# Fewer tiles transposed on TensorE in the first token steps of a two-layer mixer kernel

## The chip, the core and the metric

The kernel runs on one core of a Trainium2 chip. The metric is the device time of one execution in microseconds (us); lower is better. Engines are named as the profile names them: PE (TensorE, matrix multiply; PEld is its weight load), DVE (VectorE), ACT (ScalarE), POOL (GpSimd), and SP, whose queue (SPq) issues every DMA of this kernel in order. Each engine works through its own instructions in the order in which they were written, and waits at an instruction until what that needs is there.

## The reference

Two blocks alternate, A B A B, on x of 2048 tokens by 512 features in float32, each added to its input after a layer norm.

```python
def _A_ref(x, wqkv, wo):                 # linear attention, 32 heads of 16
    q, k, v = ...                        # from x @ wqkv
    phi = lambda t: jnp.where(t > 0, t + 1, jnp.exp(t)) + 1e-6
    pq, pk = phi(q), phi(k)
    kv = jnp.einsum("bhsd,bhse->bhde", pk, v)
    z = jnp.einsum("bhsd->bhd", pk)
    num = jnp.einsum("bhqd,bhde->bhqe", pq, kv)
    den = jnp.einsum("bhqd,bhd->bhq", pq, z)[..., None] + 1e-6
    return ... (num / den) ... @ wo

def _B_ref(x, w_in, w_sp, b_sp, w_out):  # gated mixer over tokens
    z = _gelu(jnp.einsum("bsd,df->bsf", x, w_in))
    z1 = z[..., :Fh]
    z2 = _layernorm(z[..., Fh:], axis=-1)
    g = jnp.einsum("ts,bsf->btf", w_sp, z2) + b_sp[None, :, None]
    return jnp.einsum("bsf,fd->bsd", z1 * g, w_out)
```

## The kernel before

The tokens are cut into 16 tiles of 128 rows (NT). Every float32 matrix product is made of three matmuls: each operand is split into a high half (a rounded copy, made on ScalarE, L119) and a low half (the rest, a subtraction on VectorE, L122); `mm3` (L133 to L135) multiplies high by high, high by low, and low by high. The low half of the left operand is first read by the third matmul.

The schedule is written out by hand: the order of the calls is the order of the instructions on each engine. Each of the two layers (A and then B) has three phases: P1 (keys, queries and the sum over tokens), a short transition, P2 (queries times the summed matrix, first residual, the layer norm and the two input projections of B), and P4 (the product over tokens and the output projection). The change is in P2.

P2 runs in steps s = 1 to 18; in a step several tiles are at different stages. For a tile i:

- `a(i)` multiplies the query features with the summed keys on GpSimd (L571); `a2_den` forms the denominators on VectorE (L583 to L585); `a2_mul` divides (VectorE, L592). The result is the q tile. `qturn.store(i)` then takes it on its way to be transposed.
- `b_high(i)` and `b_low(i)` get the transposed q tile and split it (L119, L122).
- `c(i)` is the matmul group that multiplies it with the 512 x 512 matrix W2: 12 matmuls. `c2` adds x (VectorE, L624), `c_stats` takes mean and variance (VectorE L196 and L198, then three small GpSimd instructions, L200 to L203), and `c3` stores x, normalises it on ScalarE (L209) and hands the y row to `xturn.store(i)`.
- `d_high(i)` and `d_low(i)` get the transposed y row and split it.
- `e(i)` multiplies it with half of the input weights: 24 matmuls. `e2` applies the gelu (ScalarE, L679), `e3` takes the statistics of z (VectorE), `e4` normalises z one step later (ScalarE).
- `f()`, twice a step, is one of seven products for four tiles at a time (12 matmuls each). The first four tiles have to be through `d` before the first `f`, so these begin in step 6.

Step s has the tiles b(s), c(s-1), d(s-2), e(s-3). PE runs c, then e, then the f units. What e(s-3) reads was made by d in step s-1, and what c(s-1) reads by b in step s-1.

A tile is transposed in one of two ways, chosen by class `Turn` (L224 to L262). If the tile's number is in `by_pe`, `get` transposes it on TensorE: four 128 x 128 transposes (L221) into one PSUM bank. A q tile (`always=True`) is first copied on ScalarE into the order of features that this needs (L240). If the number is not in `by_pe`, `store` writes the tile to DRAM in blocks (L245), `load` reads it back in another order (L249, which the profile shows as L115), and `get` turns the 32 x 32 blocks on VectorE (L260). A load waits on SP until its store has landed.

The two turns of a layer are `qturn` for the q tiles and `xturn` for the y rows (L557). The order of the calls in a step depends on both:

```python
if s in self.qturn.by_pe:
    self.c(s - 1); self.b_high(s); self.c2(s - 1); self.b_low(s); self.c_stats(s - 1)
    ...                                  # d(s - 2); late products of P1
    self.c3(s - 1); self.a2(s + 2)
    ...
else:
    self.b_high(s); self.a2_den(s + 2); self.b_low(s)
    self.c(s - 1); self.c2(s - 1); self.c_stats(s - 1)
    self.a2_mul(s + 2)
    late = s - 2 in self.xturn.by_pe     # then d(s - 2) before c3, otherwise after a
    self.c3(s - 1); self.a(s + 3)
```

`p1.late()`, called in the first form of a step, makes the query product of a tile that P1 left over; two of the six are left when P2 begins, and are made in steps 1 and 2. The pieces of the weights of f (`w1.piece`, ScalarE L119 and GpSimd L127) are split one in each step.

Of the kernel before, what the change touches and what calls it, by code (L numbers as in the profile page):

```python
# [71 lines left out]
def mixer_kernel(ctx: ExitStack, tc: tile.TileContext, x_in, wqkv, wo_d, win1_d, win2_d, wsp_d, bsp_d, wout_d,  # L72
# [64 lines left out]
    class Weight:  # L137


        def __init__(self, slots, shape, pieces, turned=False):  # L140
            self.slots, self.shape, self.pieces, self.turned = slots, shape, pieces, turned
            self.h = self.l = None
            self.raw = deque()
            self.n_load = self.n_split = 0
# [40 lines left out]
    def w_in1():  # L185
        return Weight(bigs, [P, NF, 4, P], [win1_d[f] for f in range(NF)])
# [365 lines left out]
    class P2:  # L552
        def __init__(self, p1):
            self.L = L = p1.L
            self.p1 = p1
            self.win1, self.win2 = w_in1(), p1.win2
            self.qturn, self.xturn = Turn(f"qt{L}", range(5), True), Turn(f"yt{L}", range(4))  # L557
            self.qp, self.qT, self.x, self.ms, self.xB, self.z, self.zms = {}, {}, {}, {}, {}, {}, {}
            self.fq = deque()
            self.fnext = []  # L560
# [568 lines left out]
```

## Time and profile before

| | us |
|---|---|
| median of 3 runs (lowest, highest) | 1401.97 (1400.98, 1402.58) |
| the profiled execution, device time | 1402.18 |
| its span, first to last instruction | 1400.1 |
| PE busy in the span | 1390.0 |
| mean granted TensorE clock | 0.999 |

A row of a timeline gives the start in us from the start of the span, the duration in us, the engine, the line of the kernel, the operation, what it writes and reads with the shapes, and a count; in brackets stands how long the engine had been idle before it, and what ended that. A row of windows gives, for each engine in the stretch, its busy time and the number of instructions, then the granted clock as a share, the busy share of the DMA engines and GB/s. A row of waits gives who waited for whom, the total in us, how often, and the longest. Matmuls overlap: a matmul's own duration is longer than the distance to the next, and the distance is what it costs on PE.

### The profile page before, as it was taken

Reading aid. Unit: us, or ns where it says so; the run is one execution under the profiler, and the core shown is the slowest. Engines: PE = TensorE matmul, PEld = TensorE weight load, DVE = VectorE, ACT = ScalarE, POOL = GpSimd, SP = SyncE. Lnnn points to the kernel's source line nnn. Section 1 sums busy time; section 2 is a strip of 40 time slices with the busy share of each in tenths; the row PEclk is TensorE's granted clock in tenths of the full one; section 3 lists DMA queues with packets and bytes.
Section 4 is the critical chain, followed back from the end, with each engine's and each line's share of the span. In section 5 each row is a group of like instructions: output and inputs, shape, how many; then the busy total and the mean of one; then the engine's idle time right before and its main releaser. Section 6 shows DMA issues by size and latency. Waiting matters only on the chain.

```text
span 1400.1 us, 17475 instructions
## 1 busy us (share of the span) xinstructions
PE 1390.0 (99%) x6270; PEld 1162.0 (83%) x6270; DVE 878.8 (63%) x1275; ACT 571.9 (41%) x871; POOL 399.9 (29%) x490
## 2 busy tenths in 40 slices
PE   9999999999999999999999999999999999999998
PEld 7778888888888888888888888888888888888887
DVE  6876776763477665584567767776425466666632
ACT  6675544343332332341357655444333333333420
POOL 4533345544357001041023334432100030022300
PEclk9999999999999999999999999999999999999999
DMA  6652167776897434452744413555335354434432
GB/s 233 192 151 76 61 180 239 259 240 204 300 332 264 134 120 136 165 180 98 233 127 151 129 53 112 169 186 160 112 117 158 100 167 134 133 120 167 152 111 93
DMA packets 142455, 225.69 MB, mean 161 GB/s; under 512 B 11936, under 2 KB 50592, under 8 KB 142368
## 3 DMA queue, kind: packets, MB, share of 16 engines
q1 hardware_dynamic: 142368, 224.57, 49.2%
q8 instruction: 49, 0.80, 0.3%
q14 instruction: 38, 0.31, 0.1%
HBM read 156.63 MB, written 67.90 MB: 160 GB/s over the span
## 4 chain that ended last, share of the span: by engine, by line
PE 83%; DMA 1%; DVE 0%; ACT 0%; SPq 0%; issue 0%; POOL 0%; POOLq 0%
PE bank L135 15%; PE bank L134 15%; PE bank L133 15%; PE bank L917 13%; PE bank L916 13%; PE bank L918 13%; DMA pg<-in_x_dram 1%; PE bank L221 0%; SPq L115 0%; DVE qd L122 0%; ACT qd L119 0%; DVE st L196 0%; ACT z_z L209 0%; SPq L791 0%; DVE pg L1011 0%
## 5 line engine op out<-in xcount | busy, mean ns | idle before, releaser
L918 PE MATMUL bank<-qd,pg 128*128 128x512 f32 x800 | 311.2, 389 | 0.0
L916 PE MATMUL bank<-qd,pg 128*128 128x512 f32 x800 | 311.2, 389 | 0.0
L917 PE MATMUL bank<-qd,pg 128*128 128x512 f32 x800 | 311.2, 389 | 0.0
L855 DVE TENSOR_TENSOR qd<-qd,qd 128x1024 fp32r<-128x1024 f32 x112 | 152.2, 1359 | 177.3 <-ACT qd L854 177.2
L854 ACT ACTIVATE qd<-qd 128x1024 fp32r<-128x1024 f32 x112 | 118.5, 1058 | 215.6 <-PE bank L918 198.9
L943 POOL TENSOR_TENSOR bg<-bg,pg 128x512 f32<-128x512 f32 x56 | 85.5, 1562 | 408.8 <-DVE bg L970 195.4
L916 PEld LDWEIGHTS bank<-qd,pg 128*128 128x128 f32 x800 | 150.1, 188 | 31.6
L918 PEld LDWEIGHTS bank<-qd,pg 128*128 128x128 f32 x800 | 150.2, 188 | 31.1
L917 PEld LDWEIGHTS bank<-qd,pg 128*128 128x128 f32 x800 | 150.1, 188 | 30.9
L135 PE MATMUL bank<-qd,pg 128*128 128x512 f32 x384 | 150.4, 392 | 0.1
L200 POOL TENSOR_SCALAR rs<-mv 128x1 f32<-128x1 f32 x96 | 37.4, 390 | 374.0 <-DVE mv L198 370.5
L209 ACT ACTIVATE pg<-pg,nb,rs 128x512 f32<-128x512 f32 x63 | 51.1, 810 | 181.8 <-POOL nb L203 181.7
L133 PE MATMUL bank<-qd,pg 128*128 128x512 f32 x288 | 112.8, 392 | 1.4 <-ACT pg L119 1.4
L134 PE MATMUL bank<-qd,pg 128*128 128x512 f32 x288 | 112.3, 390 | 0.0
L796 POOL TENSOR_TENSOR pg<-pg,pg 128x512 f32<-128x512 f32 x56 | 82.2, 1468 | 48.4 <-DMA pg<-in_wsp_dram 42.1
L133 PE MATMUL bank<-bg,qd 128*128 128x448 f32 x256 | 94.2, 368 | 1.0 <-ACT qd L119 1.0
L135 PE MATMUL bank<-bg,qd 128*128 128x448 f32 x256 | 93.7, 366 | 0.1
L134 PE MATMUL bank<-bg,qd 128*128 128x448 f32 x256 | 93.6, 366 | 0.0
L135 PE MATMUL bank<-qd,bg 128*128 128x512 f32 x224 | 87.5, 390 | 0.0
L134 PE MATMUL bank<-qd,bg 128*128 128x512 f32 x224 | 87.4, 390 | 0.0
L133 PE MATMUL bank<-qd,bg 128*128 128x512 f32 x224 | 87.2, 389 | 0.0
L133 PE MATMUL bank<-wo,qd 128*128 128x512 f32 x224 | 87.1, 389 | 0.0
(128 smaller groups left out, 2585.8 us busy)
## 6 DMA issues: line engine op xcount, KB each, us to landing
qd<-s SPq DMA_DIRECT2D x64, 512.0 KB, 3.4
qd<-in_wsp_dram SPq DMA_DIRECT2D x48, 512.0 KB, 3.8
pg<-x SPq DMA_DIRECT2D x64, 256.0 KB, 3.1
z<-pg SPq DMA_DIRECT2D x56, 256.0 KB, 2.5
pg<-in_wsp_dram SPq DMA_DIRECT2D x56, 256.0 KB, 4.7
s<-pg SPq DMA_DIRECT2D x56, 256.0 KB, 4.5
pg<-z SPq DMA_DIRECT2D x56, 256.0 KB, 5.4
x<-pg SPq DMA_DIRECT2D x48, 256.0 KB, 2.6
```

What stands on the lines that cost most here:

```text
L133: nc.tensor.matmul(out, ah, bh, start=start, stop=False)
L134: nc.tensor.matmul(out, ah, bl, start=False, stop=False)
L135: nc.tensor.matmul(out, al, bh, start=False, stop=stop)
L200: nc.gpsimd.tensor_scalar(rs, mv[:, 1:2], LN_EPS, None, op0=OP.add)
L209: nc.scalar.activation(y, x, AF.Identity, bias=nb, scale=rs)
L796: nc.gpsimd.tensor_tensor(t, a, b, op=OP.add)
L854: nc.scalar.activation(w[:, 0], r, AF.Copy)
L855: nc.vector.tensor_sub(w[:, 1], r, w[:, 0].bitcast(F32))
L916: m(out, h[:, o], w[:, 0, j, :], start=start, stop=False, skip_group_check=True)
L917: m(out, h[:, o], w[:, 1, j, :], start=False, stop=False, skip_group_check=True)
L918: m(out, l[:, o], w[:, 0, j, :], start=False, stop=stop, skip_group_check=True)
L943: nc.gpsimd.tensor_tensor(u, u, z1, op=OP.mult)
```

## The change

```diff
--- before.py
+++ after.py
@@ -554,7 +554,7 @@
             self.L = L = p1.L
             self.p1 = p1
             self.win1, self.win2 = w_in1(), p1.win2
-            self.qturn, self.xturn = Turn(f"qt{L}", range(5), True), Turn(f"yt{L}", range(4))
+            self.qturn, self.xturn = Turn(f"qt{L}", range(3), True), Turn(f"yt{L}", range(2))
             self.qp, self.qT, self.x, self.ms, self.xB, self.z, self.zms = {}, {}, {}, {}, {}, {}, {}
             self.fq = deque()
             self.fnext = []
```

In each layer q tiles 3 and 4 and y rows 2 and 3 go through DRAM and VectorE where before they were transposed on TensorE. Over the two layers that takes 32 transposes off TensorE and four copies (L240) off ScalarE, and adds eight block transposes (L260) on VectorE and sixteen DMAs (eight stores, eight loads) on SP's queue. Steps 3 and 4 take the second form of the step, in which `b` and the denominators come ahead of `c2` on VectorE, and `d(2)` and `d(3)` come after `c3` and `a`. The late products of P1 are still made in steps 1 and 2.

## Prediction

> **What bounds the kernel now.** The page first: TensorE (PE) is busy for nearly the whole span, and the chain that ended last runs through it.
>
> ```profile
> span 1400.1 us, 17475 instructions
> PE 1390.0 (99%) x6270; PEld 1162.0 (83%) x6270; DVE 878.8 (63%) x1275; ACT 571.9 (41%) x871; POOL 399.9 (29%) x490
> PE 83%; DMA 1%; DVE 0%; ACT 0%; SPq 0%; issue 0%; POOL 0%; POOLq 0%
> ```
>
> Then the waits of PE, in total 6.1 us (columns: total, times, longest):
>
> ```profile
> PE bank L408 <- DVE pg L403: 2.3, 1, 2.3
> PE bank L133 <- ACT z_h L119: 1.4, 1, 1.4
> PE bank L133 <- ACT pg L119: 1.4, 4, 0.6
> PE bank L133 <- ACT qd L119: 1.0, 1, 1.0
> ```
>
> So work taken off PE shortens the run, and a microsecond for which PE waits anew lengthens it, because nothing downstream has slack to take it up; only the last row lies behind the change. Next the windows of the token steps 3 to 6 of the first layer's second phase (a step starts with matmul group c; columns: PE, PEld, DVE, ACT, POOL busy):
>
> ```profile
> 161.34:169.80 8.46, 8.46 (x45) 7.59 (x44) 6.44 (x13) 4.06 (x7) 3.61 (x5) 1.00 0.35 119
> 169.80:178.29 8.49, 8.49 (x46) 7.59 (x44) 7.37 (x15) 4.57 (x7) 4.85 (x10) 1.00 0.46 116
> 178.29:186.42 8.13, 8.13 (x42) 7.15 (x41) 6.15 (x12) 4.34 (x7) 4.87 (x7) 1.00 0.59 177
> 186.42:199.52 13.10, 13.10 (x62) 11.26 (x61) 10.03 (x19) 3.85 (x6) 5.74 (x10) 1.00 0.46 142
> ```
>
> PE never stops there, but steps 3 to 5 last it only 8.1 to 8.5 us; from step 6 on, two f units are added and a step is 13.1 us. VectorE (DVE) shows its own beat:
>
> ```profile
> 167.73 0.68 DVE L624 TENSOR_TENSOR pg<-pg,bank 128x512 f32<-128x512 f32 x1
> ...
> 175.22 0.64 DVE L624 TENSOR_TENSOR pg<-pg,bank 128x512 f32<-128x512 f32 x1
> ...
> 182.88 1.08 DVE L260 STREAM_TRANSPOSE pg<-pg 128x512 f32<-128x512 f32 x1
> ...
> 193.38 1.09 DVE L260 STREAM_TRANSPOSE pg<-pg 128x512 f32<-128x512 f32 x1
> ...
> 204.41 1.06 DVE L260 STREAM_TRANSPOSE pg<-pg 128x512 f32<-128x512 f32 x1
> ```
>
> With the turns on TensorE, a step's round through VectorE, GpSimd and ScalarE is 7.5 us (167.73 to 175.22), shorter than PE's step. With the DRAM form it is 10.50 us, and 11.03 us once the y row is turned that way too. The change puts the long round into steps 3 to 5, the short ones on PE. That is the argument; the rest is its size.
>
> **Part 1, transposes removed.** Two q tiles and two y rows, four transposes each, in two layers: 32.
>
> ```profile
> L221 PE MATMUL bank<-ident,pg x84: 270/272/273, 6.3 to 873.2; 128*128 128x128 f32 x84
> ...
> 172.55 1.03 PE L221 MATMUL bank<-ident,pg 128*128 128x128 f32 x8
> 173.34 0.45 PE L133 MATMUL bank<-bg,qd 128*128 128x448 f32 x1
> ...
> 181.03 0.60 PE L221 MATMUL bank<-ident,pg 128*128 128x128 f32 x4
> 181.38 0.45 PE L133 MATMUL bank<-bg,qd 128*128 128x448 f32 x1
> ```
>
> One lasts 272 ns, but they overlap: eight hold the next matmul back 0.79 us, four 0.35 us. Per layer step 3 loses 0.44 (eight become four), step 4 loses 0.79, step 5 loses 0.35: 1.58 us, 3.2 us in all. The Trainium skill (TensorE: Matmul & The Clock Gate, Part 4: PE-mode transpose) gives about 275 ns in a kernel's context; the duration agrees with the row, but charged at that price the 32 would bring 8.8 us and the total below would be about 1408.6; the spacing decides.
>
> **Part 2, what the DRAM form puts in their place.** From step 5 of before (L260 at t = 182.88):
>
> ```profile
> 184.46 1.13 DVE L584 TENSOR_TENSOR den<-den,zeps 128x32 f32<-128x32 f32 x1
> ...
> 185.90 0.63 DVE L122 TENSOR_TENSOR pg<-pg,pg 128x512 fp32r<-128x512 f32 x1
> ...
> 187.88 0.18 DVE L198 BATCH_NORM_AGGREGATE mv<-st 128x2 f32<-128x6 f32 x1
> ...
> 189.77 0.82 ACT L209 ACTIVATE pg<-pg,nb,rs 128x512 f32<-128x512 f32 x1 [4.66 <-POOL nb L203]
> ...
> 201.64 0.69 DVE L122 TENSOR_TENSOR qd<-pg,qd 128x512 fp32r<-128x512 f32 x1 [1.51 <-ACT qd L119]
> ```
>
> The low half of the q tile is ready at t + 3.65 (185.90 + 0.63), the statistics end at L198, t + 5.00, the normalise L209 comes 1.89 later, and the low half of the y row (step 6: 201.64 + 0.69 against t = 193.38) is ready at t + 8.95. L584 takes 1.13 us here because GpSimd's L127 runs from 184.25 to 185.54; undisturbed it is 0.19 us, and the chain 0.92 us shorter:
>
> ```profile
> 171.03 0.19 DVE L584 TENSOR_TENSOR den<-den,zeps 128x32 f32<-128x32 f32 x1
> ...
> 167.69 1.30 POOL L127 TENSOR_TENSOR bg<-pg,bg 128x512 fp32r<-128x512 f32 x1 [2.96 <-ACT bg L119]
> 184.25 1.29 POOL L127 TENSOR_TENSOR bg<-pg,bg 128x512 fp32r<-128x512 f32 x1
> ```
>
> PE's pieces: group c has 12 matmuls and takes 2.74 us (178.29 to 181.03), group e has 24 and takes 4.95 us (173.34 to 178.29). The low half is first read by the third matmul, 0.46 us into c and 0.41 us into e.
>
> *Step 3.* Where VectorE is when it starts:
>
> ```profile
> 165.31 0.63 ACT L240 ACTIVATE pg<-pg 128x512 f32<-128x512 f32 x1 [0.97 <-DVE pg L592]
> 165.85 0.58 ACT L327 ACTIVATE z_q<-bank 128x512 f32<-128x512 f32 x1
> 166.46 0.63 ACT L328 ACTIVATE z_q<-z_q 128x512 f32<-128x512 f32 x1
> ...
> 167.12 0.69 DVE L329 SCALAR_TENSOR_TENSOR z_q<-bank,z_q 128x512 f32<-128x512 f32 x1 [1.85 <-ACT z_q L328]
> ...
> 171.20 0.82 ACT L209 ACTIVATE pg<-pg,nb,rs 128x512 f32<-128x512 f32 x1 [2.61 <-POOL nb L203]
> ```
>
> ScalarE's copy L240 of q tile 4 is gone, and with it its 0.97 us wait and 0.54 us of its own, so L329 moves from 167.12 to 165.6, and L260 starts at 166.2. L127 also moves 1.5 us ahead and ends at 167.5, before L584 is reached at 167.8: the short chain. Low half at 166.2 + 3.65 - 0.92 = 168.93; PE wants it at 169.36 + 0.46, no wait, with 0.9 us to spare. L198 at 170.28, L209 at 172.17, and by before's 4.02 us from L209 to the next step (171.20 to 175.22, the table load of the gelu in it) step 4 starts at 176.19.
>
> *Step 4* (t = 176.19): q low half at 179.84, so c starts 179.38 where PE, at 169.36 + 7.70, asks for it at 177.06: 2.32 us of waiting. c ends 182.12. y row 2 low half at 185.14, e starts 184.73: 2.61 us. e ends 189.68.
>
> *Step 5* (t = 176.19 + 11.03 = 187.22): q at 190.87, c starts 190.41: 0.73 us. c ends 193.15. y row 3 at 196.17, e starts 195.76: 2.61 us, e ends 200.71. In before this e ended at 186.42 + 2.74 + 4.95 = 194.11.
>
> *From step 6 on* PE's step of 13.1 us exceeds VectorE's 11.03, so nothing is added; nothing comes back either, but for one wait of before:
>
> ```profile
> 216.49 0.47 PE L133 MATMUL bank<-bg,qd 128*128 128x448 f32 x1 [1.04 <-ACT qd L119]
> ```
>
> VectorE's round is then 187.22 + 11.03 - 193.38 = 4.9 us later, PE 6.6 us: this 1.04 us of the first layer goes.
>
> **Part 3, the transfers.** Sixteen more DMAs, a store and a load for each tile, in SP's order, where the load waits until the store has landed, and weight and x loads stand behind it.
>
> ```profile
> 173.03 0.38 SPq L245 DMA_DIRECT2D qt<-pg  x1
> ...
> 175.73 0.33 SPq L115 DMA_DIRECT2D pg<-qt  x1
> ...
> DMA to landing us min/median/max: 2.3/3.4/6.4
> ```
>
> Tile 4, multiplied by 165.3, is stored at once, its load goes out 2.7 us later at 168.0 and lands by 171.4 at the median, 174.4 at the worst: before its L260 at 176.2. Row 2, normalised at 173.0, lands by 179 or, at the worst, 182.1; wanted at 176.19 + 5.7 = 181.9. I cost them at nothing; the cover is the late VectorE itself, and without it a tile would add at most the 6.4 - 3.4 = 3 us between worst and median. The queued weight and x loads have a full step before their users.
>
> **The sum.** The second layer's step 4 has the same window as the first's, 8.48 us against 8.49:
>
> ```profile
> 861.63:870.11 8.48, 8.48 (x45) 7.59 (x44) 7.36 (x15) 4.57 (x7) 4.85 (x10) 1.00 0.47 128
> ```
>
> So in each layer e of step 5 ends 6.6 us later (waits of 8.27 less 1.58 of transposes, rounding aside). 2 x 6.6 - 1.04 = 12.2 us. The profiled execution took 1402.18 us with its span of 1400.1; the median is 1401.97. Forecast 1414.
>
> Bounds of the unknown: if L127 misses L584 in steps 4 and 5 also, 2 x 0.92 per layer less, 1410; if it hits it in step 3, 0.92 per layer more, 1416; the worst landing adds up to 3 us a layer, 1420. I take the rows' own pattern because step 5's neighbours repeat it.
>
> **Rivals.** *All hidden (faster):* the round through VectorE fits, and only the transposes go: 1401.97 - 3.2 = 1398.8, with the 1.04 us wait left. For it: PE runs ahead through steps 3 to 5 with no wait now, and L240 leaves ScalarE. Against it: 10.5 us does not go into 8.1. *Partly hidden:* waits of step 4 alone, say half: 1402 + 6 = 1408; it needs y rows ready earlier than t + 8.95, for which no row speaks. *The round trip decides:* a load lands after VectorE asks, 3 us more a layer and up: 1420; the row 2 margin is only 0.3 us at the worst. *A slow TensorE clock after the gaps:*
>
> ```profile
> L408 PE MATMUL bank<-pg,ones x14: 391/572/794, 2.3 to 7.4; 128*128 128x512 f32 x14
> ```
>
> After the idle start matmuls took 572 ns in the median against 391; 14 such after each of six gaps over 2 us is 14 x 0.18 x 6 = 15 us: 1429. Against it: the granted clock stays 1.00 round the 1.04 us wait. The Trainium skill (TensorE: Matmul & The Clock Gate, Part 1: The HAM clock gate) has the clock halved after an idle window of about 3.4 us; by that rule gaps of 2.6 us keep it, and no trace here shows such a gap in mid-run.
>
> **How the numbers follow.** Forecast 0.67, partly hidden 0.11, all hidden 0.09, round trip 0.09, clock 0.04. Range 1405 to 1420: it takes in the bounds and the partly hidden case, and leaves out the first rival and the clock. A difference under 0.2% (2.8 us) can't be told from none: faster 0.09, same 0.04 (the thin edge of the partly hidden), slower 0.87.
>
> **What would show it.** In the profile after: 32 fewer L221 on PE, 8 more L260; in the PE waits, new rows of 0.7 to 2.6 us, eight in all, for pg L119 or L122 (q) and qd L119 or L122 (y), in steps 4 and 5 of each layer; steps 4 and 5 some 10 to 11 us long, step 3 about 8.0, step 6 13.1; clock 1.00. I am wrong if L260 waits for DMA in steps 3 to 5 (round trip), if PE's waits stay at 6.1 us (all hidden), or if steps after 6 lengthen too.

## The result and the profile after

The changed kernel takes 1413.01 us (median of 6 runs, 1412.09 to 1413.72), the kernel before 1402.28 (6 runs, 1400.98 to 1405.49): a ratio of 1.0074, 95% interval 1.0064 to 1.0085, or 10.7 us slower. The forecast was 1414, its range 1405 to 1420.

The page of the profiled execution after (1413.72 us), first its head, then the waits of PE (columns: total, times, longest):

```profile
span 1411.8 us, 17426 instructions
PE 1393.9 (99%) x6238; PEld 1163.2 (82%) x6238; DVE 888.5 (63%) x1283; ACT 570.8 (40%) x867; POOL 400.7 (28%) x490
```

```profile
PE bank L133 <- ACT qd L119: 6.7, 4, 2.0
...
PE bank L135 <- DVE pg L122: 2.3, 2, 1.2
```

PE has 32 matmuls less and a span 11.7 us longer. The row of qd L119 (a y row, e) has gone from one wait of 1.0 to four with 6.7 us, and pg L122 (the low half of a q tile, c) is new. "99% busy" did not move: a share over the whole span doesn't show 12 us.

The windows of PE in the first layer, cut where the matmul groups c(2), c(3), c(4), c(5) and the first f start; the last row ends where the f units of the next step begin (columns as in the windows of before: busy time and count of PE, PEld, DVE, ACT and POOL, granted clock, DMA share, GB/s):

```profile
163.01:171.04 8.03, 8.03 (x42) 7.16 (x40) 7.55 (x15) 3.57 (x6) 3.62 (x5) 1.00 0.61 170
171.04:179.07 8.03, 7.77 (x38) 6.58 (x36) 4.69 (x10) 4.23 (x6) 4.09 (x8) 1.00 0.56 184
179.07:192.19 13.12, 9.96 (x37) 7.82 (x37) 10.64 (x18) 4.36 (x7) 5.76 (x9) 0.87 0.54 184
192.19:201.82 9.63, 8.11 (x37) 6.61 (x36) 7.01 (x12) 4.37 (x7) 4.80 (x8) 1.00 0.51 157
201.82:214.90 13.08, 13.08 (x62) 11.32 (x61) 10.58 (x19) 5.34 (x9) 5.08 (x9) 1.00 0.58 188
```

Two things stand here. The stretches of c(4) with e(2) and of c(5) with e(3), before 8.13 and 7.6 us (the f units left out), are 13.12 and 9.63; from the first f to the f units of the next step it is 13.1, as long as a step of before. And the granted clock is 0.87 over the third row, which the forecast had at 1.00.

The rows of VectorE and PE behind this (timeline; start, duration, engine, line, operation):

```profile
167.27 1.10 DVE L260 STREAM_TRANSPOSE pg<-pg 128x512 f32<-128x512 f32 x1
...
177.27 1.08 DVE L260 STREAM_TRANSPOSE pg<-pg 128x512 f32<-128x512 f32 x1
...
178.86 1.10 DVE L584 TENSOR_TENSOR den<-den,zeps 128x32 f32<-128x32 f32 x1
...
180.26 0.63 DVE L122 TENSOR_TENSOR pg<-pg,pg 128x512 fp32r<-128x512 f32 x1
...
188.27 1.05 DVE L260 STREAM_TRANSPOSE pg<-pg 128x512 f32<-128x512 f32 x1
...
193.93 1.08 DVE L260 STREAM_TRANSPOSE pg<-pg 128x512 f32<-128x512 f32 x1
```

```profile
179.07 0.50 PE L133 MATMUL bank<-qd,pg 128*128 128x512 f32 x1 [0.26 <-ACT pg L119]
...
180.94 0.50 PE L135 MATMUL bank<-qd,pg 128*128 128x512 f32 x1 [1.14 <-DVE pg L122]
...
185.52 0.47 PE L133 MATMUL bank<-bg,qd 128*128 128x448 f32 x1 [2.02 <-ACT qd L119]
```

The q tiles 3, 4 and 5 are turned at 167.27, 177.27 and 188.27: rounds of 10.0 and 11.0 us, where before a step's round was 7.5. PE begins c(4) as soon as the high half is there and stops at the third matmul until the low half (180.26 + 0.63) is; e(2) waits 2.02 us for y row 2. The groups of the two kinds of transposes:

```profile
L221 PE MATMUL bank<-ident,pg x52: 269/272/421, 6.7 to 861.9; 128*128 128x128 f32 x52
...
L260 DVE STREAM_TRANSPOSE pg<-pg x83: 1035/1081/1121, 29.9 to 1027.1; 128x512 f32<-128x512 f32 x83
...
  DMA pg<-yt: 3.1, 2
```

32 fewer on PE and 8 more on VectorE, as the change says; the waits of L260 for a y row's load stay at two with 3.1 us (before 3.0), and no wait of L260 for a DMA lies in the changed steps of either layer, so none of the eight new ones waited for its load.

### The profile page after: what moved, and what is told of

The parts are those of the page before. It is cut to its first block, busy times and chain, and to the rows that moved or that the text cites. A ratio compares the mean times of both kernels' runs of the same rounds, so it can differ in the third digit from the quotient of the medians.

```text
span 1411.8 us, 17426 instructions
## 1 busy us (share of the span) xinstructions
PE 1393.9 (99%) x6238; PEld 1163.2 (82%) x6238; DVE 888.5 (63%) x1283; ACT 570.8 (40%) x867; POOL 400.7 (28%) x490
## 5 line engine op out<-in xcount | busy, mean ns | idle before, releaser
L916 PEld LDWEIGHTS bank<-qd,pg 128*128 128x128 f32 x800 | 150.2, 188 | 31.4
L917 PEld LDWEIGHTS bank<-qd,pg 128*128 128x128 f32 x800 | 150.2, 188 | 31.2
L918 PEld LDWEIGHTS bank<-qd,pg 128*128 128x128 f32 x800 | 150.2, 188 | 30.9
L200 POOL TENSOR_SCALAR rs<-mv 128x1 f32<-128x1 f32 x96 | 38.7, 403 | 387.5 <-DVE mv L198 387.4
L133 PE MATMUL bank<-bg,qd 128*128 128x448 f32 x256 | 95.3, 372 | 6.7 <-ACT qd L119 6.7
L796 POOL TENSOR_TENSOR pg<-pg,pg 128x512 f32<-128x512 f32 x56 | 83.0, 1483 | 45.8 <-DMA qd<-in_wsp_dram 18.9
L135 PE MATMUL bank<-bg,qd 128*128 128x448 f32 x256 | 95.3, 372 | 0.2
L134 PE MATMUL bank<-bg,qd 128*128 128x448 f32 x256 | 94.9, 371 | 0.0
L260 DVE STREAM_TRANSPOSE pg<-pg 128x512 f32<-128x512 f32 x83 | 89.5, 1078 | 6.8 <-DMA pg<-yt 3.1
L135 PEld LDWEIGHTS bank<-qd,pg 128*128 128x128 f32 x384 | 72.4, 188 | 20.7 <-DVE pg L122 5.8
L135 PE MATMUL bank<-qd,bg 128*128 128x512 f32 x224 | 87.5, 391 | 0.0
L134 PE MATMUL bank<-qd,bg 128*128 128x512 f32 x224 | 87.5, 390 | 0.0
```

Of the source, the lines that this page charges most:

```text
L133: nc.tensor.matmul(out, ah, bh, start=start, stop=False)
L134: nc.tensor.matmul(out, ah, bl, start=False, stop=False)
L135: nc.tensor.matmul(out, al, bh, start=False, stop=stop)
L260: nc.vector.transpose(y.rearrange("p c (t m) -> p m c t", m=4), r.rearrange("p (m c j) -> p m c j", m=4, c=4))
L796: nc.gpsimd.tensor_tensor(t, a, b, op=OP.add)
L916: m(out, h[:, o], w[:, 0, j, :], start=start, stop=False, skip_group_check=True)
```

## Experiments

Each run stands against the kernel before on the same chip (1401.75 to 1402.43 us). In the diffs a minus line is the changed kernel's, if not said otherwise.

**1 and 2. The q tiles alone, the y rows alone** (the minus line is that of the kernel before).

```diff
-Turn(f"qt{L}", range(5), True), Turn(f"yt{L}", range(4))
+Turn(f"qt{L}", range(3), True), Turn(f"yt{L}", range(4))    # q_only
+Turn(f"qt{L}", range(5), True), Turn(f"yt{L}", range(2))    # y_only
```

> Only the q tiles 3 and 4 go through DRAM (three q tiles on TensorE), the four y rows stay on TensorE. Theory (the VectorE, GpSimd and ScalarE round of a step in the DRAM form, 10.5 us, is longer than PE's step of about 8 us): PE waits for q tiles 4 and 5 and the first f unit of a layer starts some 3 us later than before; 1402.3 + 2 x 3 = about 1408. Rival A (the DRAM round trip decides): the q trips landed 3 to 5 us before they were used in the changed kernel, so only eight transposes a layer less and no waits, about 1400.5. Rival B (not the turns but the order of the second form of the step decides): steps 3 and 4 take that form here as in the changed kernel, about 1413.

> Only the y rows 2 and 3 go through DRAM (two y rows on TensorE), five q tiles stay on TensorE and steps 3 and 4 keep the first form. Theory: VectorE's step 4 grows by the block transpose and its wait for ScalarE, about 1.5 us, and y row 3 in step 5 is ready only 8.95 us into the step; PE waits about 2 us for q tile 5 and 2.6 us for y row 3 in each layer, in all about 1402.3 + 2 x 4 - 1 = 1409. Rival A (DRAM round trip): row 2 is wanted at once when it lands, 1409 to 1415, and L260 waits for a DMA. Rival B (order of the second form): steps 3 and 4 are in the first form, so only transposes go, about 1401.

Measured: q_only 1408.59 (1407.58 to 1408.96; ratio 1.0034 to 1.0059), y_only 1407.04 (1405.49 to 1408.61; 1.0022 to 1.0047). Each half costs, 6.5 and 4.9 us, and the sum, 11.4, is about the whole, 10.7. y_only came a little below its forecast. The waits of PE in y_only are those of the y rows and of the low half of q tile 5. In the first layer the L260 of that tile starts 0.4 us later than in before (183.32 against 182.88), and PE reaches c(5) 1.0 us sooner (185.40 against 186.42):

```profile
PE bank L133 <- ACT qd L119: 4.0, 2, 2.0
...
PE bank L135 <- DVE pg L122: 2.0, 2, 1.0
```

**3. The round trip through DRAM.** For q tiles 3 and 4 and y rows 2 and 3 the store and the load are left out (16 DMAs), and L260 reads the tile where it lies. Left out of the computation is the exchange of blocks between partitions.

```diff
 # a2_mul
+            if i in (3, 4):
+                self.qturn.raw[i] = self.qp.pop(i).rearrange("p h d -> p (h d)")
+                self.qturn.page[i] = t
+                return
 # c3
+            if i in (2, 3):
+                self.xturn.raw[i] = self.xturn.page[i] = y
+                return
```

> The changed kernel without the DRAM trips of q tiles 3 and 4 and y rows 2 and 3: the block transpose on VectorE reads the tile where it lies, so the exchange of blocks between partitions is left out for these tiles, and so are the 16 DMAs. Theory: the transfers cost nothing, the time stays at 1413 (within 1 us). Rival A (the DRAM round trip or SP's queue decides): PE's new waits go, about 1399 to 1403.

Measured: 1412.86 (1412.22 to 1413.73; ratio 1.0066 to 1.0092), as with the trips. The transfers cost nothing that shows here; the rival of the round trip falls.

**4. The first form of the step for steps 3 to 5**, with the same tiles on PE as after the change. Step 5 had the second form before the change too, so it moves as well.

```diff
-                if s in self.qturn.by_pe:
+                if s < 6:
```

> The changed kernel with steps 3 to 5 in the first form of the step (c2 and the statistics ahead of the denominators, d ahead of c3), the turns through DRAM as changed. Theory with this refinement: what counts is how late the statistics and the low halves come in VectorE's order; with the denominators behind them the round is about 8.2 us, q tile 5 and y row 3 are ready about when PE asks for them, the waits shrink from 4.6 us a layer to under 1, and the time is about 1399 to 1403. If the amount of VectorE's work in the step decides, whatever its order, the round stays about 10.5 us and the time 1411 to 1413. If the DRAM round trip decides, y rows land too late for the earlier place, L260 waits for DMA by 1 to 3 us a step, 1408 or more.

Measured: 1405.03 (11 runs, 1403.97 to 1405.92; ratio 1.0012 to 1.0030), between the expectations: 8 us of the 10.7 hang on the order of the calls in these three steps, and some 3 are left. Waits of PE and the timeline of VectorE and GpSimd in this kernel:

```profile
PE bank L135 <- DVE qd L122: 3.2, 4, 0.8
...
PE bank L135 <- DVE pg L122: 1.5, 2, 0.7
```

```profile
173.57 1.08 DVE L260 STREAM_TRANSPOSE pg<-pg 128x512 f32<-128x512 f32 x1
...
175.35 1.43 DVE L122 TENSOR_TENSOR pg<-pg,pg 128x512 fp32r<-128x512 f32 x1 [0.18 <-ACT pg L119]
...
179.28 1.44 DVE L122 TENSOR_TENSOR qd<-pg,qd 128x512 fp32r<-128x512 f32 x1 [0.70 <-ACT qd L119]
...
183.88 1.06 DVE L260 STREAM_TRANSPOSE pg<-pg 128x512 f32<-128x512 f32 x1
```

```profile
174.94 1.30 POOL L127 TENSOR_TENSOR bg<-pg,bg 128x512 fp32r<-128x512 f32 x1
...
178.89 1.28 POOL L571 TENSOR_TENSOR pg<-z_q,pg 128x512 f32<-128x512 f32 x1
```

The round is still 10.3 us (173.57 to 183.88), yet PE waits less: the low half of the q tile now ends 3.2 us after the tile's L260 began (175.35 + 1.43) instead of 3.6, that of the y row 7.15 (179.28 + 1.44) instead of 8.9 (185.50 + 0.69 against 177.27 in the changed kernel). Two low halves of 1.4 us in place of 0.63 to 0.69 stand out: each overlaps a GpSimd instruction and ends about 0.5 us after it. Run 10 moves one of the two GpSimd instructions away.

**5. Less work on VectorE.** The denominators of tiles 5 to 7 are left out (a2_den does nothing), and those tiles are divided by tile 4's.

```diff
-            if i >= NT:
+            if i >= NT or i in (5, 6, 7):
```

> The changed kernel without the denominators (three small VectorE instructions) of tiles 5, 6 and 7, which stand in steps 3, 4 and 5 between the block transpose and the low half; these tiles are divided by tile 4's denominators instead. Theory (VectorE's round decides): the round loses 1.2 us in step 3 and, with the collision with GpSimd, about 2.1 us in steps 4 and 5, PE's waits in each layer shrink from about 4.6 to under 1 us, time about 1402 to 1404. If the DRAM trips or the form of the step decide: 1413.

Measured: 1410.25 (1409.82 to 1411.06; ratio 1.0047 to 1.0072), a miss. VectorE in this kernel:

```profile
175.19 1.08 DVE L260 STREAM_TRANSPOSE pg<-pg 128x512 f32<-128x512 f32 x1
176.96 1.42 DVE L122 TENSOR_TENSOR pg<-pg,pg 128x512 fp32r<-128x512 f32 x1 [0.70 <-ACT pg L119]
...
185.76 1.03 DVE L260 STREAM_TRANSPOSE pg<-pg 128x512 f32<-128x512 f32 x1
```

The denominators, 1.9 us between the end of L260 and the low half in the changed kernel (177.27 + 1.08 to 180.26), are gone, but the low half then waits 0.70 us for ScalarE's high copy and is the next to overlap L127, and the round is 10.57 us in place of 11.00. It is a chain of hand-offs between VectorE, ScalarE and GpSimd; taking work from one link shortens it only down to the next.

**6. The price of the transposes on PE.** The kernel before, with those 32 transposes made twice.

```diff
-        for c in range(4):
+        for c in list(range(4)) * (2 if twice else 1):
```

> The kernel before, with the 32 transposes in question each made twice, into the same place (the result is the same). It prices a transpose on PE where PE never waits: at the spacing in the trace (0.79 us for eight, about 0.1 us each) 32 more cost 3.2 us, 1405.5; at the 275 ns of the Trainium skill (TensorE: Matmul & The Clock Gate, Part 4: PE-mode transpose) 8.8 us, 1411; if they were hidden, 1402.3.

Measured: 1404.34 (11 runs, 1403.46 to 1404.92; ratio 1.0009 to 1.0027), 2.45 us more. By the starts of PE's groups, the stretch from c(2) to the first f takes 34.46 us in place of 32.71 in the first layer and as much more in the second: 1.75 us for 16 transposes, 3.5 us in all, 0.11 us for each, near the spacing (3.2 us in all). The total shows less because the old wait of 1.04 us for qd L119 is gone in this run's PE waits. The 275 ns that the prediction quoted from the Trainium skill (TensorE: Matmul & The Clock Gate, Part 4: PE-mode transpose) would be 8.8 us.

**7 and 8. Late products of P1 as cover.** DEFER sets how many query products P1 leaves to be made in P2, on PE: 9 in place of 6. In defer9_first steps 3 to 5 have the first form (as in 4); in defer9_second the second form, with the late products called there.

```diff
-DEFER = 6
+DEFER = 9
```

> The kernel of order6 (changed turns, steps 3 to 5 in the first form), and three more of P1's query products (tiles 7 to 9) put off until steps 3 to 5 of P2, one in each, so that PE has 2.7 us more to do there without any more work in all. Theory: PE's steps 3 to 5 grow to about 10.5 us, as long as VectorE's round of 10.3 plus 0.6, the waits shrink to about 0.5 us a step and the saved transposes show: 1399 to 1402. If P1 loses what P2 gains (its last steps wait for VectorE instead), 1403 to 1408.

> The changed kernel (steps 3 to 5 in the second form), with the same three query products put off until steps 3 to 5. Theory: PE's steps of about 10.5 us against VectorE's round of 11.0 plus 0.6 leave about 1 us a step, time 1401 to 1406. If P1 loses what P2 gains, 1407 to 1412. If longer steps on PE don't help, 1413.

Measured: defer9_first 1413.22 (ratio 1.0066 to 1.0093), defer9_second 1433.82 (1.0212 to 1.0240); both miss. In defer9_first the loss lies in P1, which now waits for its own split operands:

```profile
PE bank L133 <- ACT z_h L119: 9.3, 7, 1.8
```

That was one wait of 1.4 us before. c(2) of the first layer starts only 0.9 us sooner than in before (160.45 against 161.34), though three query products of 2.7 us less stand ahead of it. In defer9_first no wait of PE is left between 163 and 207 us: longer steps cover the round, but the matmuls were taken from where they were needed. In defer9_second P1 loses as much, but the larger part is lost in P2: PE waits 14.9 us for y rows there, and one gap of PE is 6.7 us. The late products' own chain (L327 and L328 on ScalarE, with two table loads of 1.28 us in each of steps 4 and 5, and L329 on VectorE) makes the round from q tile 4 to q tile 5 16.7 us (192.44 - 175.71).

**9 and 10. Without the weight pieces (L119, L127) in steps 2 to 4**, which go to steps 5 and 6; once in the changed kernel, once with the first form.

```diff
-                w1.piece(True)
-                w1.fetch()
+                for _ in range({1: 1, 5: 2, 6: 2, 7: 1, 8: 1}.get(s, 0)):
+                    w1.piece(True)
+                for _ in range({1: 1, 5: 2, 6: 2}.get(s, 0)):
+                    w1.fetch()
```

> The changed kernel with the pieces of f's weights (a ScalarE copy and the GpSimd subtraction L127 each) made one in step 1, none in steps 2 to 4, two in steps 5 and 6, one in steps 7 and 8, so that no L127 runs in steps 3 to 5. Theory, revised after no_den (the round is a chain of hand-offs between VectorE, ScalarE and GpSimd, in which a VectorE instruction with two SBUF inputs waits for a GpSimd one that is under way): L584 drops from 1.1 to 0.2 us in steps 4 and 5, the statistics come 0.9 us sooner in each, and the first f unit of a layer starts about 1.8 us sooner: 1413 - 3.6 = 1409 to 1410. If the collision is hidden, as the denominators turned out to be: 1412 to 1413. Rival (the amount of VectorE's work decides): 1413.

> order6 with the same places for the weight pieces. In order6 the low half of the q tile takes 1.43 us in place of 0.69 in steps 4 and 5, while L127 runs. Theory: each round is 0.75 us shorter, PE's waits of about 2.3 us a layer shrink to under 1, 1401.5 to 1403. If the collision is hidden: 1405.

Measured: after_nopiece 1411.86 (1409.92 to 1413.15; ratio 1.0052 to 1.0076), 1.1 us below the changed kernel with ranges that overlap: inconclusive. Its profile says more. L584 takes 0.19 us in steps 4 and 5, and from c(2) to the first f PE needs 36.9 us in either layer, where the changed kernel needs 38.8: 1.9 us less, and the theory expected 1.8. What the two layers win is lost behind the changed steps of the first: PE waits 1.45 and 1.02 us there for y rows (at 221.07 and 246.16) that the changed kernel does not wait for, and its lag behind the kernel before grows from 4.2 us at the first f to 6.4 at the second layer's c(2), where that of the changed kernel shrinks by 2.1. order6_nopiece 1407.41 (1407.05 to 1408.24; 1.0023 to 1.0049), 2.4 us worse than order6, a miss in the total. There too the stretch from c(2) to the first f is shorter, 33.7 us in place of 35.0. Its timeline of GpSimd and of PE shows what was traded:

```profile
206.82 2.54 POOL L127 TENSOR_TENSOR bg<-pg,bg 128x512 fp32r<-128x512 f32 x2
213.84 2.65 POOL L798 TENSOR_TENSOR pg<-pg,pg 128x512 f32<-128x512 f32 x2 [4.48 <-PE bank L135]
216.58 0.22 POOL L200 TENSOR_SCALAR rs<-mv 128x1 f32<-128x1 f32 x1
```

```profile
219.24 0.47 PE L133 MATMUL bank<-bg,qd 128*128 128x448 f32 x1 [2.74 <-ACT qd L119]
```

L798 (L796 in the other kernels), which adds token weights, starts at 213.84 (210.85 in order6); the row statistics L200 queue behind it on GpSimd, and the y row is 2.74 us late for PE. The row names PE as what L798 waited for; in before the same addition waits for the load of those weights, which here stands behind two weight loads on SP's queue. Which of the two it was is not settled.

**11. The first form with the y rows back on PE**: only q tiles 3 and 4 go through DRAM.

```diff
-Turn(f"qt{L}", range(3), True), Turn(f"yt{L}", range(2))
+Turn(f"qt{L}", range(3), True), Turn(f"yt{L}", range(4))
...
-                if s in self.qturn.by_pe:
+                if s < 6:
```

> Only the q tiles 3 and 4 through DRAM, the four y rows on TensorE, and steps 3 to 5 in the first form. Theory: without a block transpose of a y row the round is about 9 us and the low halves come early in it; step 5 starts on VectorE about when it does in the kernel before, so PE does not wait in steps 3 to 5 and the 16 transposes saved in place of 32 show: 1400 to 1402. If a round longer than PE's step is all that counts, PE waits about 1 us a step: 1404 to 1408.

Measured: 1401.03 (11 runs, 1400.30 to 1402.08; ratio to before 0.9982 to 0.9999): 1.4 us below before, 12 below the change, and 7.6 below q_only, which turns the same tiles in the same places and differs in the form of steps 3 and 4 (and of 5) alone. VectorE and the waits of PE here:

```profile
174.15 1.04 DVE L260 STREAM_TRANSPOSE pg<-pg 128x512 f32<-128x512 f32 x1
...
183.16 1.05 DVE L260 STREAM_TRANSPOSE pg<-pg 128x512 f32<-128x512 f32 x1
```

```profile
PE bank L133 <- ACT qd L119: 1.0, 1, 1.0
...
PE bank L221 <- ACT pg L209: 0.2, 1, 0.2
```

A round of 9.0 us is still longer than PE's step, but PE's lead lasts for the three steps, and of new waits only 0.2 us are seen. The gain is small: the interval ends just below 1.

**12. Filling the gaps.** The changed kernel with 44 needless matmuls of 128x512, whose result nobody reads: in each layer 12 between c(3) and e(1) and 10 between c(4) and e(2), one group of matmuls earlier than the expectation says.

```diff
                 self.xturn.load(s - 1)
+                if s in (4, 5):
+                    b = banks.get(PAGE)
+                    for _ in range(12 if s == 4 else 10):
+                        nc.tensor.matmul(b, self.win2.h[:, 0, 0:P], self.W2[0][:, 0, :], start=True, stop=True)
+                    banks.put(b)
```

> The changed kernel with needless matmuls of 128x512 on TensorE whose result nobody reads: 12 after e(1), 10 after e(2), in each layer, 44 in all. At the 0.23 us from one such matmul to the next in c(3) of the changed kernel that is 5.06 us a layer, 10.1 us in all. Theory (the waits of TensorE before c(4), e(2) and e(3) last as long as the round through VectorE, whatever TensorE does meanwhile): the time stays at 1411 to 1414; the waits shrink by about what is put in, e(3) still starts when y row 3 is there, and with fewer idle stretches the granted clock stays at 1.00 and e(2) takes 4.95 us again. If the slow stretch of the clock had cost anything, the time falls by up to 2 us in spite of the work. Rival (TensorE's work always sets the time, the waits are only where it is shown): 1413 + 10 = 1423.

Measured: 1412.62 (1411.61 to 1414.94; ratio 1.0064 to 1.0091). 10.1 us of matmuls cost nothing. Rows of PE and VectorE:

```profile
171.99 2.88 PE L756 MATMUL bank<-qd,bg 128*128 128x512 f32 x12
...
182.32 2.43 PE L756 MATMUL bank<-qd,bg 128*128 128x512 f32 x10
...
194.74 0.47 PE L133 MATMUL bank<-bg,qd 128*128 128x448 f32 x1 [2.02 <-ACT qd L119]
```

```profile
175.46 1.07 DVE L260 STREAM_TRANSPOSE pg<-pg 128x512 f32<-128x512 f32 x1
...
192.15 1.07 DVE L260 STREAM_TRANSPOSE pg<-pg 128x512 f32<-128x512 f32 x1
```

e(3) starts 2.59 us after L260 of y row 3 (194.74 against 192.15; in the changed kernel the same wait of VectorE's hand-off, 2.6 us from 193.93), whatever PE has done before. From the L260 of q tile 4 to that of y row 3 it is 16.69 us (192.15 - 175.46), in the changed kernel 16.66 (193.93 - 177.27). That is the theory at its plainest: in these steps this work on PE is free, and VectorE's round sets the end. The part on the clock is a miss; it stands in the last section.

**The stage alone.** A total also holds what happens ahead of the changed steps and behind them. The stretch of PE from the start of c(2) to the first f leaves that out (us, from the starts of the matmuls in the profiled executions):

| | first layer | second layer | more than before, a layer |
|---|---|---|---|
| before | 32.7 | 32.7 | |
| the changed kernel | 38.8 | 38.8 | 6.1 |
| 1, q_only | 35.8 | 35.7 | 3.1 |
| 2, y_only | 37.0 | 35.7 | 4.3 and 3.0 |
| 3, no_trip | 38.9 | 38.9 | 6.2 |
| 4, order6 | 35.0 | 35.0 | 2.3 |
| 5, no_den | 37.7 | 37.8 | 5.0 |
| 9, after_nopiece | 36.9 | 36.9 | 4.2 |
| 10, order6_nopiece | 33.7 | 33.6 | 1.0 |
| 11, q_first6 | 32.5 | 32.5 | -0.2 |

The two halves, 3.1 and 3.0, add up to the whole. The 4.3 of y_only has a stretch of lower clock in e(3) (0.51 from 193.00 to 195.50). Run 12 is left out: its 40.4 and 40.1 hold the slow e(3) of the last section. Runs 7 and 8 move work into the stretch. The first form of the step takes away 3.8 of the 6.1, and moving the weight pieces (L119 and L127) out of the steps takes away 1.9 with the second form and 1.3 with the first.

## Why the prediction was right

**What bounds, and where.** Right: the waits are at c(4), e(2) and e(3) in each layer (the forecast had c(5) as well, see below), step 3 has none, steps from the first f on are unchanged, and runs 3 and 12 show that neither transfers nor PE's own work matter there.

**Part 1**, 3.2 us for the 32 transposes: run 6 measures 3.5.

**Part 2, the size per layer**: 6.6 us forecast, 6.1 measured. The profiled execution of the changed kernel comes into P2 1.67 us later than that of before, at an instruction that nothing in the change precedes (L592 below); in the other runs with the same P1 this point lies between 156.05 and 157.32. The late start comes from P1: behind a wait of 1.42 us, which before has too, the granted clock falls to 0.50, where in before it is 1.00 (from 98.67 to 104.00), and matmuls start 0.43 us apart in place of 0.23:

```profile
98.74 0.50 PE L133 MATMUL bank<-qd,z_h 128*128 128x512 f32 x1 [1.42 <-ACT z_h L119]
```

```profile
100.61:103.17 2.56, 2.56 (x7) 1.98 (x6) 2.46 (x4) 1.47 (x3) 1.13 (x1) 0.50 0.11 32
```

Taken off, f of the first layer is 201.82 - 194.05 - 1.67 = 6.10 later, and the second layer adds 6.09. The missing half microsecond is a part of the edit that was not counted. VectorE's divisions of q tiles 3 and 4, first before, then after:

```profile
156.78 0.69 DVE L592 SCALAR_TENSOR_TENSOR pg<-z_q,den 128x512 f32<-128x512 f32 x1
...
163.96 1.32 DVE L592 SCALAR_TENSOR_TENSOR pg<-z_q,den 128x512 f32<-128x512 f32 x1
```

```profile
158.45 0.69 DVE L592 SCALAR_TENSOR_TENSOR pg<-z_q,den 128x512 f32<-128x512 f32 x1
...
165.11 1.32 DVE L592 SCALAR_TENSOR_TENSOR pg<-z_q,den 128x512 f32<-128x512 f32 x1
```

7.18 us lie between them before, 6.66 after. The prediction took out ScalarE's copy L240 of tile 4 only; that of tile 3, one step earlier, is gone as well and brings VectorE 0.52 us forward. With VectorE's own lag of 165.11 - 163.96 = 1.15, the forecasts 166.2 (first L260), 187.22 (L260 of tile 5) and 200.71 (f) become 167.35, 188.37 and 201.86; the rows say 167.27, 188.27 and 201.82. The rest of the step's working held to 0.1 us at these points.

**The wait that comes back**: 1.04 us forecast, 2.1 measured (PE is 7.77 late at the first layer's f and 5.68 at the second layer's c(2)). The term was the idle time in one row. By the starts of the matmuls in before, the place costs more: 215.06 to 216.49 and 216.79 to 217.21, where the spacing is 0.20, and a third late operand at 240.66 to 241.07; with the wider spacing of the matmuls next to them these places come to 2.0 us, and after has no gap over 0.30 us from 210 to 260. So 1.67 + 6.10 - 2.1 + 6.1 = 11.8 is the profiled difference of the spans, 11.7; without the late start it is 10.1, beside 10.7 between the medians. The forecast of 12.2 was high by twice 0.5 and by 1.1. That the profiled difference of 11.7 comes closer to it is luck: the slow stretch in P1, which lies ahead of all that was changed, made up most of the shortfall.

**Step by step**: the wait before c(5) (0.73 forecast) did not occur, since e(2) took 6.67 us in place of 4.95 at a lower clock and PE reached c(5) late; that before e(3) was 1.46 in place of 2.61, in part for the same reason and in part because the row counts only up to the high half. In run 3, whose profiled execution has a clock of 1.00 there, c(5) does wait, and e(3) longer:

```profile
190.84 0.50 PE L135 MATMUL bank<-qd,pg 128*128 128x512 f32 x1 [0.53 <-DVE pg L122]
...
195.41 0.47 PE L133 MATMUL bank<-bg,qd 128*128 128x448 f32 x1 [2.01 <-ACT qd L119]
```

The first f is as late either way (6.2 and 6.1 us more than before), since VectorE's round sets it. Of the rivals, all hidden and partly hidden fell with the waits at all three groups, the round trip with run 3. That of the clock was half right: its mechanism happened, at a price near nothing in e(2), since PE would have waited there; the same in P1 is the 1.67 us above.

**What the prediction left unsaid.** It put the whole loss on the DRAM form of the turn. Runs 4 and 11 show that most of it is the form of the step that comes with it: `by_pe` decides not only how a tile is turned but also the order on VectorE, and with the first form in steps 3 to 5 two q tiles a layer can leave PE with a small gain. Step 5 had the second form already before the change; the kernel before with the first form there was not run, so how much of runs 4 and 11 is due to step 5 is not shown.

## What to carry to other kernels

A trade between engines is to be costed by the round that it lengthens, in the stage where it falls, not by the work removed: taking 3 us off an engine that is 99% busy made the run 10.7 longer, because another engine's chain of hand-offs was already near its step there. Where one flag picks both a method and an order of calls, try them apart. Count every copy that goes with a moved tile, also one issued a step earlier, and measure an old wait by the starts of the instructions around it, since its idle row shows only part. Compare the changed stage alone as well as the total: twice here a gain in the stage was lost behind it.

## What the hardware showed

**The clock.** Windows of the changed kernel (first layer): the stretch ahead of e(2), and the one in it:

```profile
178.64:185.52 6.88, 3.46 (x13) 2.10 (x12) 5.23 (x10) 1.76 (x4) 3.90 (x6) 1.00 0.52 183
...
186.25:189.03 2.78, 2.78 (x9) 2.48 (x9) 2.04 (x4) 1.62 (x4) 0.50 (x2) 0.50 0.29 86
```

After 6.88 us in which PE was busy for 3.46 (gaps of 1.5 and 2.4 us from start to start) the granted clock is 0.50 for about 2.8 us, and so again in the second layer. In P1 of the changed kernel a single gap of 1.8 us from start to start was enough (96.94 to 98.74, idle for 1.42; its rows stand beside Part 2), and in the run with the fillers one of 2.4 us (192.34 to 194.74); e(3) then took 6.85 us, and there it lies on the path:

```profile
196.00:199.00 3.00, 3.00 (x10) 2.65 (x9) 2.57 (x5) 1.12 (x4) 1.15 (x4) 0.50 0.31 105
```

Of its five executions the three with a mean clock of 1.000 took 1411.61 to 1412.62 us, the two at 0.997 and 0.998 took 1414.72 and 1414.94. Of the six of the changed kernel the three at 0.996 and 0.997 took 1413.48 to 1413.72, the three at 0.998 and 0.999 1412.09 to 1412.55. It does not come each time: the profiled execution of run 3 has waits of 2.0 us and a clock of 1.000, and of all the profiled executions that have the wait of 1.4 us in P1, only that of the changed kernel is slow behind it. The Trainium skill (TensorE: Matmul & The Clock Gate, Part 1: The HAM clock gate) puts the drop after an idle window of about 3.4 us; here gaps of 1.8 and 2.4 us were enough in some executions, and the measurement decides. What tells the executions apart stays open.

**VectorE beside GpSimd.** A low half that reads two tiles in SBUF takes 1.4 us when a GpSimd instruction runs beside it (run 4); the same L122 reading PSUM took 0.68 us in before at 168.33, beside L127 from 167.69. The row of before:

```profile
168.33 0.68 DVE L122 TENSOR_TENSOR pg<-bank,pg 128x512 fp32r<-128x512 f32 x1
```

The Trainium skill (GPSIMD Engine Reference, 1. Specifications) says that the two engines share SBUF interfaces and contend where a VectorE instruction has two SBUF inputs; these rows agree. So a tile turned through DRAM can cost more than its transpose: its low half, which came from PSUM before, can now meet GpSimd's traffic. In the changed kernel it is L584 that meets it, with 1.10 us in place of 0.19; run 9 takes that away, and 1.9 us a layer with it.
